# Replacing bf16 idle matmuls at the start of a kernel by about a quarter as many fp32 ones

## The chip, the cores and the metric

The kernel runs on one core of one Trainium2 chip. The metric is device time in microseconds (us) of one execution; the figure quoted is the median of several executions. The span that the profiler shows is about 2 us shorter than that time (403.2 us of 405.02 us in the profiled execution of the kernel before). Ratios and their intervals compare one kernel's fast runs with those of the kernel before in the same rounds, on the same chip, so they are not quite the ratios of the medians.

## The reference

The reference computes Linformer attention (keys and values projected from 1024 rows down to 64) and then a feed-forward layer that takes the maximum of three projections:

```python
def _attn_ref(q, k, v, E, F):            # q, k, v: (8, 8, 1024, 64); E, F: (64, 1024)
    k_proj = np.einsum('ks,bhsd->bhkd', E, k)
    v_proj = np.einsum('ks,bhsd->bhkd', F, v)
    scores = 1.0 / np.sqrt(64) * np.matmul(q, k_proj.transpose(0, 1, 3, 2))
    ...                                  # softmax over the 64 columns
    return np.matmul(attn, v_proj)

def _moe_ref(x, w1, w2, w3, w_out):      # x: (8192, 512); w1..w3: (512, 768); w_out: (768, 512)
    h = np.maximum(np.maximum(x @ w1, x @ w2), x @ w3)
    return (h @ w_out).astype(np.float32)
```

## The kernel before

Apart from `E` and `F`, which come in fp32 by DMAs of SP, everything is loaded in bf16 by DMAs that POOL issues, and PE (TensorE) does nearly all of the work. At the start PE has nothing to compute, as nothing has landed. There the kernel runs matmuls whose result nobody reads, on a zeroed tile `warm`, to keep PE active; the code calls this `idle`. Its purpose is the clock. In this kernel's trace most of the first ten idle matmuls start 0.43 us apart, and those of the second group 0.22 us apart. These two rates are called half and full speed here, and the change from the one to the other the release of the clock.

The parts that matter here, cut:

```python
warm = const.tile([P, 512], BF16, name="warm")
...
nc.vector.memset(warm, 0.0)
make_identity(nc, ident)                     # POOL builds the identity after it has issued six loads
...
def idle(n):
    t, ns = bank()
    for _ in range(n):
        nc.tensor.matmul(out=t, lhsT=warm[:, 0:P], rhs=warm, start=True, stop=True)
    free[ns[0]] = pe(n * MM)                 # the planner's clock only, no instruction
...
idle(10)                                     # the first group
at(6.3)
turn_ef()                                    # casts and transposes E and F: 8 transposes, need ident
q_duo(0)                                     # 16 transposes of q
copy("v", efT[:, :, P:P + KP], efT[:, :, KP:P])
idle(4)                                      # the second group
at(9.0)
k_duo(0)                                     # projection of k_t: 8 matmuls, needs the k_t load
idle(2)
...                                          # scores, softmax sums, further single idle matmuls
up_first(...)                                # the first up-projection, needs the w_sb load
```

The softmax here doesn't subtract the row's maximum and nothing guards it: scores larger than these inputs give would overflow.

Of the kernel before, what the change touches and what calls it, by code (L numbers as in the profile page):

```python
# [8 lines left out]
FP32 = mybir.dt.float32  # L9
# [6 lines left out]
def kernel(  # L16
# [13 lines left out]
    nc = tc.nc  # L30
# [7 lines left out]
    P = 128  # L38
# [11 lines left out]
    const = ctx.enter_context(tc.tile_pool(name="const", bufs=1))  # L50
# [14 lines left out]
    free = [0.0] * 8  # L65
# [13 lines left out]
    def bank():  # L79
        n = min(range(8), key=lambda n: free[n])  # L80
        deal((n,))
        return psum_t[:, n, :], (n,)

    def pe(dt, wait=0.0):
        clock["pe"] = max(clock["pe"], wait) + dt
        return clock["pe"]
# [9 lines left out]
    MM = 0.216  # L96

    def copy(eng, o, i, ns=(), dt=0.65):
        done = {  # L99
            "v": nc.vector.tensor_copy, "s": nc.scalar.copy, "g": nc.gpsimd.tensor_copy  # L100
        }[eng](out=o, in_=i)
        runs(eng, clock["pe"] if ns else 0.0, dt, ns)
        return done
# [14 lines left out]
    ident = const.tile([P, P], BF16, name="ident")  # L118
    ones = const.tile([P, HALF], BF16, name="ones")
    warm = const.tile([P, 512], BF16, name="warm")  # L120
    w_sb = [const.tile([P, NCT, DF], BF16, name=f"w{i}_sb") for i in range(3)]
    wout_sb = const.tile([P, NJT, DO], BF16, name="wout_sb")

# [43 lines left out]
    load_kv(2, slice(2, 4))  # L167

    nc.scalar.preload_act_table_set("natural_log_exp_and_others")
    nc.vector.memset(warm, 0.0)  # L170
    make_identity(nc, ident)
    nc.vector.memset(ones, 1.0)
# [200 lines left out]
        return f  # L373


    def idle(n):

        t, ns = bank()
        for _ in range(n):
            nc.tensor.matmul(out=t, lhsT=warm[:, 0:P], rhs=warm, start=True, stop=True)  # L380
        free[ns[0]] = pe(n * MM)

    def turn_ef():
        for i in range(2):
# [16 lines left out]
    def at(us):  # L401
        clock["pe"] = max(clock["pe"], us)
# [59 lines left out]
    def x(g):  # L462
        scale_x(0, g, *C0, values(0, g, *C0))

    idle(10)
    at(6.3)
    turn_ef()
    q_duo(0)
    copy("v", efT[:, :, P:P + KP], efT[:, :, KP:P])
    idle(4)  # L470
    at(9.0)
    k_duo(0)
    idle(2)
    kt_duo(0)
    idle(1)
# [265 lines left out]
```

## Time and profile before

| | us |
|---|---|
| time, median of 3 (range) | 405.22 (405.04 to 405.93) |
| span of the profiled execution | 403.2 |
| PE busy | 389.6 (97% of the span) |
| first idle group, ten bf16 | 1.20 to 5.38 |
| PE waits for the identity from POOL | 1.21, until 6.58 |
| second idle group, four bf16 | 7.75 to 8.79 |
| PE waits for `k_t` | 1.25, until 10.03 |
| PE waits for `w_sb` | 1.08, until 19.54 |

Two lines of the page of the kernel before: the busy time of each engine, and the chain of work that ended last, by engine.

```profile
PE 389.6 (97%) x2314; PEld 178.0 (44%) x2357; DVE 203.1 (50%) x313; ACT 189.4 (47%) x274; POOL 31.6 (8%) x44
...
PE 82%; DMA 11%; ACT 2%; POOL 1%; DVE 1%; issue 1%; DVEq 0%; ACTq 0%; POOLq 0%
```

Over the whole span PE is the limit. That average does not say what limits the first 20 us, and those are all that the change touches. The same chain in order of time, cut to 0 to 60 us; the columns are start, duration, and what the chain went through:

```profile
1.24 0.88 POOL q_t L152
...
6.48 13.01 DMA w_sb<-in_moe_w_dram
...
25.87 30.10 DMA v_t<-in_v_dram
```

In the front, the chain is POOL issuing loads, then a `w_sb` load on its way until 19.49, and once more a load of the next batch's `v_t`, which lands at 55.97. The front is bound by loads.

The timeline of PE in the front (start, duration of the whole group, engine, line, operation, count, and in brackets the idle time before it and what ended it):

```profile
1.20 4.18 PE L380 MATMUL banks<-warm 128*128 128x512 bf16 x10 [1.20 <-DVE warm L170]
6.58 0.66 PE L391 MATMUL banks<-ident,ef_b 128*128 128x128 bf16 x8 [1.21 <-POOL ident masks.py:199]
...
7.75 1.04 PE L380 MATMUL banks<-warm 128*128 128x512 bf16 x4
10.03 1.03 PE L409 MATMUL banks<-k_t,efT 128*64 128x256 bf16 x8 [1.25 <-DMA k_t<-in_k_dram]
...
19.54 1.47 PE L506 MATMUL banks<-xT,w_sb 128*128 128x512 bf16 x6 [1.08 <-DMA w_sb<-in_moe_w_dram]
```

The three waits in the brackets are gaps that lateness in front of them can use up. The eighth, ninth and tenth idle matmul, one line each:

```profile
4.16 0.63 PE L380 MATMUL banks<-warm 128*128 128x512 bf16 x1
4.58 0.57 PE L380 MATMUL banks<-warm 128*128 128x512 bf16 x1
4.99 0.38 PE L380 MATMUL banks<-warm 128*128 128x512 bf16 x1
```

They start 0.42 to 0.43 us apart until the ninth, which is followed after 0.41 us by a tenth that takes 0.38 us instead of 0.63. In the second group they are 0.22 us apart. So the clock was released to full speed just before 5 us, 3.8 us after PE's first matmul.

What comes before the first idle matmul (timeline of all engines):

```profile
0.86 0.27 DVE L170 MEMSET warm<- 128x256 uint32 x1 [0.86 <-PEq L725]
...
1.24 0.88 POOL L152 DMA_DIRECT2D q_t<-in_q_dram  x1 [0.79 <-POOLq L725]
```

DVE's memset of `warm` lasts from 0.86 to 1.13 us, and POOL issues its first load at 1.24.

### The profile page before, as it was taken

The page shows a single profiled execution, that of the slowest core. Times are in us where ns is not written, and L with a number is a line of the kernel's source. Part 1 is how long each engine was busy: PE and PEld are TensorE (multiplying, and loading weights), DVE is VectorE, ACT ScalarE, POOL GpSimd, SP SyncE. Part 2 cuts the span into 40 slices and gives each one's busy share as a digit, 9 for nine tenths or more (in the row PEclk, how much of TensorE's full clock was granted, in tenths as well). Part 3 has the DMA queues.
Part 4 walks back from the last instruction along what each step waited for, and adds up shares of the span by engine and source line. Part 5 has one row for each costly group of instructions (what it writes and reads, how often), then busy time and mean ns, then how long its engine had stood idle before and what let it go on. Part 6 is the DMA issues. An engine that isn't in the chain of part 4 may idle for free.

```text
span 403.2 us, 5841 instructions
## 1 busy us (share of the span) xinstructions
PE 389.6 (97%) x2314; PEld 178.0 (44%) x2357; DVE 203.1 (50%) x313; ACT 189.4 (47%) x274; POOL 31.6 (8%) x44
## 2 busy tenths in 40 slices
PE   6799999999999999999999999999999999999996
PEld 2444444344444435444544445444544444444443
DVE  2338755761764527537353655626364363525251
ACT  2622537525672376555643555437535555432322
POOL 7340001001000100100100002000000000000000
PEclk9999999999999999999999999999999999999999
DMA  9999999959907994991799029950510202020202
GB/s 150 206 205 207 232 201 165 235 128 187 227 0 216 191 220 106 155 243 20 211 178 216 24 40 236 204 148 0 147 63 2 104 2 104 2 104 0 106 0 105
DMA packets 62667, 53.33 MB, mean 132 GB/s; under 512 B 30128, under 2 KB 58288, under 8 KB 62640
## 3 DMA queue, kind: packets, MB, share of 16 engines
q0 software_dynamic: 28512, 28.31, 44.3%
q1 hardware_dynamic: 33984, 24.51, 19.7%
q8 instruction: 18, 0.29, 0.3%
q10 hardware_dynamic: 144, 0.13, 0.1%
q14 instruction: 9, 0.07, 0.1%
HBM read 57.15 MB, written 16.78 MB: 183 GB/s over the span
## 4 chain that ended last, share of the span: by engine, by line
PE 82%; DMA 11%; ACT 2%; POOL 1%; DVE 1%; issue 1%; DVEq 0%; ACTq 0%; POOLq 0%
PE banks L506 56%; PE banks L603 18%; DMA v_t<-in_v_dram 7%; PE banks L220 4%; DMA w_sb<-in_moe_w_dram 3%; PE banks L284 3%; PE banks L200 2%; DVE xT L250 1%; ACT zi L239 1%; ACT zl L233 1%; DMA out_dram<-o_sb 0%; POOL k_t L147 0%; POOL q_t L152 0%; POOL v_t L147 0%; PE banks L435 0%
## 5 line engine op out<-in xcount | busy, mean ns | idle before, releaser
L506 PE MATMUL banks<-xT,w_sb 128*128 128x512 bf16 x1119 | 254.9, 379 | 3.7 <-DMA w_sb<-in_moe_w_dram 1.1
L506 PEld LDWEIGHTS <-w_sb 128*128 128x128 bf16 x1152 | 109.4, 98 | 138.1 <-issue 10.7
L568 DVE TENSOR_TENSOR m<-banks,h1s 128x512 f32<-128x512 f32 x90 | 62.1, 690 | 84.4 <-ACT h1s L564 52.2
L564 ACT COPY h1s<-banks 128x512 f32<-128x512 f32 x90 | 52.5, 583 | 90.3 <-PE banks L506 88.2
L603 PE MATMUL banks<-wout_sb,hT 128*128 128x512 bf16 x370 | 84.6, 379 | 0.8 <-issue 0.5
L250 DVE TENSOR_TENSOR xT<-banks,zi 128x1024 bf16<-128x1024 f32 (+1 forms) x36 | 39.8, 1106 | 73.6 <-ACT zi L239 54.2
L516 DVE TENSOR_TENSOR hT<-banks,m 128x512 bf16<-128x512 f32 x90 | 62.3, 692 | 10.4 <-PE banks L506 1.2
L99 ACT COPY o_sb<-banks 128x512 f32<-128x512 f32 (+1 forms) x56 | 32.6, 581 | 52.2 <-PE banks L603 52.1
L603 PEld LDWEIGHTS <-hT 128*128 128x128 bf16 x378 | 36.0, 98 | 45.2 <-issue 3.1
L233 ACT ACTIVATE zl<-banks 128x1024 f32<-128x1024 f32 (+1 forms) x36 | 33.5, 930 | 31.4 <-PE banks L220 30.5
L211 ACT ACTIVATE pT<-banks 128x1024 bf16<-128x1024 f32 (+1 forms) x36 | 33.2, 930 | 15.6 <-PE banks L200 15.6
L239 ACT ACTIVATE zi<-zl 128x1024 f32<-128x1024 f32 (+1 forms) x36 | 34.6, 962 | 1.1
L189 POOL DMA_DIRECT2D q_t<-in_q_dram x7 | 6.2, 880 | 201.0 <-DMA qT<-q_p 70.6
L220 PE MATMUL banks<-pT,ones 64*64 64x512 bf16 (+1 forms) x144 | 13.7, 374 | 0.7 <-DVE xT L250 0.3
L220 PE MATMUL banks<-pT,vp 64*64 64x512 bf16 (+1 forms) x144 | 13.3, 355 | 0.7 <-DVE vp L99 0.6
L200 PE MATMUL banks<-qT,kpT 64*64 64x512 bf16 (+1 forms) x144 | 13.3, 358 | 0.6 <-DVE m L568 0.3
L284 PEld LDWEIGHTS <-efT 128*64 128x64 bf16 x224 | 11.6, 110 | 3.3 <-issue 2.7
L99 DVE CAST vp<-banks 64x256 bf16<-64x256 f32 (+1 forms) x18 | 7.1, 397 | 7.4 <-ACT vp L99 3.7
L220 PEld LDWEIGHTS <-ones 64*64 64x64 bf16 x144 | 4.4, 103 | 14.3 <-issue 14.2
L99 DVE COPY q_p<-q_t 128x1024 bf16<-128x1024 bf16 x28 | 10.0, 419 | 0.0
L99 ACT CAST vp<-banks 64x256 bf16<-64x256 f32 x14 | 5.1, 365 | 8.8 <-PE banks L284 8.6
L380 PE MATMUL banks<-warm 128*128 128x512 bf16 x19 | 7.0, 498 | 1.2 <-DVE warm L170 1.2
(48 smaller groups left out, 102.5 us busy)
## 6 DMA issues: line engine op xcount, KB each, us to landing
out_dram<-o_sb SPq DMA_DIRECT2D x30, 512.0 KB, 3.4
q_t<-in_q_dram POOLq DMA_DIRECT2D x7, 1024.0 KB, 9.6
k_t<-in_k_dram POOLq DMA_DIRECT2D x7, 1024.0 KB, 14.0
v_t<-in_v_dram POOLq DMA_DIRECT2D x7, 1024.0 KB, 18.8
w_sb<-in_moe_w_dram POOLq DMA_DIRECT2D x5, 384.0 KB, 12.4
k_t<-in_k_dram POOLq DMA_DIRECT2D x2, 512.0 KB, 9.1
v_t<-in_v_dram POOLq DMA_DIRECT2D x4, 256.0 KB, 12.2
wout_sb<-in_moe_w_out_dram POOLq DMA_DIRECT2D x1, 768.0 KB, 15.7
```

What stands on the lines that cost most here:

```text
L99: done = {"v": nc.vector.tensor_copy, "s": nc.scalar.copy, "g": nc.gpsimd.tensor_copy}[eng](out=o, in_=i)
L211: nc.scalar.activation(out=pTs[b, g, lo], in_=t, func=AF.Exp, scale=scale)
L220: nc.tensor.matmul(out=t[hp * HALF:(hp + 1) * HALF, c, 0:nsi * HALF], lhsT=w(rows, hp), rhs=p[rows, hp, :], start=True, stop=True,)
L233: nc.scalar.activation(out=zl, in_=t, func=AF.Ln)
L239: nc.scalar.activation(out=zi, in_=zl, func=AF.Exp, scale=-1.0)
L250: nc.vector.tensor_tensor(out=xTs[b][:, g, lo:lo + nsi, :].rearrange("a (c s) p -> a c (s p)", c=2), in0=t, in1=zi, op=ALU.mult,)
L284: nc.tensor.matmul(out=t[hh * HALF:(hh + 1) * HALF, 0:width], lhsT=efT[:, si, (kv - 1) * KP:kv * KP], rhs=qkv[b][kv][:, heads[hh], si, :], ...
L506: nc.tensor.matmul(out=h, lhsT=w_sb[i][:, ct, jt * P:(jt + 1) * P], rhs=xTs[b][:, ct, ch * SPC:(ch + 1) * SPC, :], start=(ct == first), st ...
L516: nc.vector.tensor_tensor(out=o, in0=h, in1=other, op=ALU.max)
L564: nc.scalar.copy(out=h1s, in_=h[0][0])
L568: nc.vector.tensor_tensor(out=m12, in0=h[1][0], in1=h1s, op=ALU.max)
L603: nc.tensor.matmul(out=o_ps, lhsT=hTs[b, ch][:, jt, tt * P:(tt + 1) * P], rhs=wout_sb[:, jt, :], start=(jt == 0), stop=(jt == NJT - 1),)
```

## The change

The idle matmuls at the front become fp32 ones, about a quarter as many. The intent is to keep PE as active with fewer instructions. The changed planner counts an fp32 one as four bf16 ones. No trace of the kernel before has an fp32 matmul; the profile after shows one at half speed as two instructions 0.85 us apart, so about 1.7 us, four times the 0.43 us of a bf16 one. Ten become three (as long as 12 bf16 ones) and four become one (as long as 4). The later idle matmuls stay bf16, so both tiles are needed, and the new memset stands first.

```diff
+    warm_f = const.tile([P, 512], FP32, name="warm_f")
 ...
+    nc.vector.memset(warm_f, 0.0)
     nc.vector.memset(warm, 0.0)
 ...
-    def idle(n):
+    def idle(n, w=warm):
 ...
-            nc.tensor.matmul(out=t, lhsT=warm[:, 0:P], rhs=warm, start=True, stop=True)
-        free[ns[0]] = pe(n * MM)
+            nc.tensor.matmul(out=t, lhsT=w[:, 0:P], rhs=w, start=True, stop=True)
+        free[ns[0]] = pe(n * MM * (4 if w is warm_f else 1))
 ...
-    idle(10)
+    idle(3, warm_f)
 ...
-    idle(4)
+    idle(1, warm_f)
```

## The prediction

> **What bounds the kernel now.** The median is 405.22 us (405.04 to 405.93), the span 403.2 us. The page has PE busy 389.6 us (97%), and the chain that ended last is 82% PE. But the edit touches only the first 9 us, and there the chain is not PE: it runs through POOL issuing loads (1.24 to 6.24 us, with the identity build at its end), then the DMA of a `w_sb` piece (6.48 to 19.49). Then the first up-projection matmul starts (19.54, after PE idled 1.08 us). So the front is bound by loads.
>
> **What the idle matmuls do now (timeline).** Ten bf16 128x512 from `warm` run from 1.20 to 5.38. They start 0.43 us apart (weight loads at 1.60, 2.03 ... 4.59), nine of about 0.61 us; the last must be about 0.38 us, as the mean is 600 ns. So the array reached full speed near 5.0 us. The PEclk row (1.00 throughout) doesn't show this. PE then waits 1.21 us for the identity from POOL and starts the transposes at 6.58. Four more idle matmuls run 7.75 to 8.79, about 0.22 us apart. PE then waits 1.25 us for `k_t` (10.03).
>
> **What the change does.**
> - DVE gets one more memset, 128x512 fp32, in front. The 128x256 one took 0.272 us and 128x64 took 0.112: about 0.83 ns an element, so 0.49 us by estimate. The first idle matmul starts at 1.41 to 1.5 instead of 1.20. POOL's first load issue (1.24) should not move.
> - 3 fp32 matmuls replace 10, 1 replaces 4. [...]
> - With the release after as much activity as now (3.8 us, near 5.2 us), three finish near 6.1, range 5.7 to 6.6[...].
> - Nothing else moves; the bank order is unchanged.
>
> **Critical path.** Ending by 6.58 costs nothing. Ending at 7.9 delays transposes and `efT` copies by 1.3 us, about all of the 1.24 us wait for `k_t`. Anything left meets the 1.08 us wait before 19.54. Filling the gap from 5.4 to 6.6 buys nothing: the clock is already full by 5.0. I expect 0.0 us of effect on the path, give or take 0.5 us of DMA timing.
>
> **Prediction: 405.3 us, 80% range 404.5 to 406.2.** Faster by over 2%: 0.01; within 2%: 0.98; slower by over 2%: 0.01.
>
> **What would show it.** Right: the first fp32 matmul at 1.4 to 1.5, spans of about 1.7 us then shorter, transposes at 6.6 to 7.0 with full-speed durations (eight in about 0.66 us), the first `k_t` matmul at 10.0, the first up-projection matmul at 19.5, and the stretch from 20 us on unchanged. Wrong: transposes or `k_t` projection at twice their duration (fp32 passes don't release the clock), POOL's first issue later than 1.24 (the memset holds it up, which shifts the loads).
>
> **What would make it wrong.** If the clock isn't released by fp32 activity, everything up to some 10 us runs slower, up to 2 us by estimate, about half hidden behind the `w_sb` wait: 406 to 407 us.

Three fp32 matmuls of about 1.7 us at half speed, begun at 1.41 to 1.5 us and sped up by a release near 5.2, finish near 6.1 us. The upper case is the end at 7.9 us under "Critical path".

## The result and the profile after

The changed kernel took 405.28 us (median of 5, 405.19 to 405.52), and the kernel before took 405.29 us (median of 5, 405.04 to 405.93). The ratio is 0.9998 with a 95% interval from 0.9984 to 1.0013: the same.

The page of the changed kernel, same lines as before:

```profile
PE 394.5 (98%) x2351; PEld 178.5 (44%) x2351; DVE 203.5 (50%) x314; ACT 189.4 (47%) x274; POOL 31.6 (8%) x44
...
PE 82%; DMA 11%; ACT 2%; DVE 1%; POOL 1%; issue 1%; DVEq 0%; ACTq 0%; POOLq 0%
```

PE's busy sum is 4.9 us higher at the same time, and this must not be read as more work. The page before counts 1119 up-projection matmuls and 1152 weight loads for them, so some matmul records are missing there.

The memset and POOL's first issue (timeline of all engines):

```profile
0.92 0.48 DVE L171 MEMSET warm_f<- 128x512 f32 x1 [0.92 <-PEq L727]
...
1.25 0.88 POOL L153 DMA_DIRECT2D q_t<-in_q_dram  x1 [0.80 <-POOLq L727]
```

The new memset takes 0.48 us and ends at 1.40. POOL's first issue stays at 1.25: the memset holds up nothing but the idle matmuls.

PE in the front, with the lines that answer to those before:

```profile
1.46 5.28 PE L382 MATMUL banks<-warm_f 128*128 128x512 f32 x6 [1.46 <-DVE warm_f L171]
6.58 0.66 PE L393 MATMUL banks<-ident,ef_b 128*128 128x128 bf16 x8
...
7.74 1.12 PE L382 MATMUL banks<-warm_f 128*128 128x512 f32 x2
9.90 1.03 PE L411 MATMUL banks<-k_t,efT 128*64 128x256 bf16 x8 [1.04 <-DMA k_t<-in_k_dram]
...
19.50 1.47 PE L508 MATMUL banks<-xT,w_sb 128*128 128x512 bf16 x6 [1.18 <-DMA w_sb<-in_moe_w_dram]
```

There are two lessons in the first line. Three fp32 matmuls are six records: each fp32 matmul runs as two instructions. And the group ends at 6.74, after the first transpose has begun, so it fills the 1.21 us wait for the identity to its end. From the transposes on, all is as it was: 6.58, 7.74, then `k_t` at 9.90, and the first up-projection matmul at 19.50 (19.54 before). Single records of the first group:

```profile
4.18 1.06 PE L382 MATMUL banks<-warm_f 128*128 128x512 f32 x1
5.03 1.06 PE L382 MATMUL banks<-warm_f 128*128 128x512 f32 x1
5.89 0.85 PE L382 MATMUL banks<-warm_f 128*128 128x512 f32 x1
```

Instructions of the group start 0.85 us apart, twice the 0.43 us of a bf16 one, up to the last; that one begins at 5.89, and the first transpose follows 0.69 us later. The clock was therefore released in the sixth instruction, near 6.4 us, not near 5. The chain, in order of time, is the one from before:

```profile
6.48 12.97 DMA w_sb<-in_moe_w_dram
...
25.95 30.06 DMA v_t<-in_v_dram
```

### The profile page after: what moved, and what is told of

Read it like the earlier page. It is cut to its first block, busy times and chain, and to the rows that moved or that the text cites. A ratio compares the mean times of both kernels' runs of the same rounds, so it can differ in the third digit from the quotient of the medians.

```text
span 403.5 us, 5873 instructions
## 1 busy us (share of the span) xinstructions
PE 394.5 (98%) x2351; PEld 178.5 (44%) x2351; DVE 203.5 (50%) x314; ACT 189.4 (47%) x274; POOL 31.6 (8%) x44
## 4 chain that ended last, share of the span: by engine, by line
PE 82%; DMA 11%; ACT 2%; DVE 1%; POOL 1%; issue 1%; DVEq 0%; ACTq 0%; POOLq 0%
PE banks L508 56%; PE banks L605 18%; DMA v_t<-in_v_dram 7%; PE banks L222 4%; DMA w_sb<-in_moe_w_dram 3%; PE banks L286 3%; PE banks L202 2%; ACT zi L241 1%; DVE xT L252 1%; ACT zl L235 1%; DMA out_dram<-o_sb 0%; POOL k_t L148 0%; POOL q_t L153 0%; POOL v_t L148 0%; DVE m L570 0%
## 5 line engine op out<-in xcount | busy, mean ns | idle before, releaser
L508 PE MATMUL banks<-xT,w_sb 128*128 128x512 bf16 x1152 | 257.9, 379 | 1.5 <-DMA w_sb<-in_moe_w_dram 1.2
L605 PE MATMUL banks<-wout_sb,hT 128*128 128x512 bf16 x378 | 85.7, 379 | 0.1
L99 DVE COPY o_sb<-banks 128x512 f32<-128x512 f32 (+1 forms) x9 | 5.8, 654 | 4.5 <-DMA out_dram<-o_sb 4.5
```

What stands on the lines that cost most here:

```text
L99: done = {"v": nc.vector.tensor_copy, "s": nc.scalar.copy, "g": nc.gpsimd.tensor_copy}[eng](out=o, in_=i)
L508: nc.tensor.matmul(out=h, lhsT=w_sb[i][:, ct, jt * P:(jt + 1) * P], rhs=xTs[b][:, ct, ch * SPC:(ch + 1) * SPC, :], start=(ct == first), st ...
L605: nc.tensor.matmul(out=o_ps, lhsT=hTs[b, ch][:, jt, tt * P:(tt + 1) * P], rhs=wout_sb[:, jt, :], start=(jt == 0), stop=(jt == NJT - 1),)
```

## The experiments

Theory A, the prediction's: both kernels release the clock in time, and the front has slack because it waits for loads, so nothing of the change is on the path. Its rivals:

- B: there is no slack, every microsecond of idle matmul counts, and the tie is two effects that cancel.
- C (named in the expectation of fp32_x8): the front does not matter at all, as later load waits absorb whatever happens there.
- E: these idle matmuls are worth nothing, whatever their type.
- D: fp32 matmuls count for less as activity, so fp32 releases the clock later (6.4 against 5.0 us above).
- F: the release point differs from execution to execution, and the two points above are chance.

In every experiment the planner's clock values were kept, so that the order of all other work and its PSUM banks stay those of the changed kernel (before_again is the kernel before itself). Each kernel gave correct results. "Before" was timed on the same chip: its medians were 405.54 us (11 runs), 404.97 (9) and 405.07 (11). Kernels are compared only within the same rounds.

| run | first, second group | median us (range) | ratio to before, 95% interval |
|---|---|---|---|
| fp32_x8 | 8 fp32, 1 fp32 | 407.27 (406.94 to 408.49) | 1.0046 (1.0028 to 1.0064) |
| bf16_x32 | 32 bf16, 1 fp32 | 407.97 (406.87 to 408.40) | 1.0053 (1.0035 to 1.0071) |
| no_front | none, none | 407.00 (406.13 to 408.85) | 1.0038 (1.0016 to 1.0060) |
| fp32_x2 | 2 fp32, 1 fp32 | 406.03 (405.50 to 406.39) | 1.0008 (0.9991 to 1.0025) |
| before_again | 10 bf16, 4 bf16 | 405.12 (404.99 to 405.31) | 1.0000 (0.9986 to 1.0013) |
| after_again | 3 fp32, 1 fp32 | 405.35 (405.22 to 406.56) | 1.0010 (0.9996 to 1.0023) |
| bf16_x12 | 12 bf16, 4 bf16 | 405.48 (405.17 to 405.68) | 1.0007 (0.9995 to 1.0020) |
| fp32_x4 | 4 fp32, 1 fp32 | 405.50 (405.39 to 406.61) | 1.0014 (1.0001 to 1.0026) |
| no_front_again | none, none | 406.73 (406.04 to 407.21) | 1.0032 (1.0016 to 1.0047) |
| no_first | none, 1 fp32 | 405.77 (405.32 to 406.50) | 1.0011 (0.9995 to 1.0028) |
| no_second | 3 fp32, none | 406.19 (405.22 to 409.01) | 1.0032 (1.0004 to 1.0060) |
| bf16_x12_again | 12 bf16, 4 bf16 | 405.72 (405.18 to 406.19) | 1.0003 (0.9987 to 1.0020) |

### Is there slack? Eight fp32 ones, and the same work as bf16

```diff
-    idle(3, warm_f)
+    idle(8, warm_f, plan=12)        # run fp32_x8; plan: what the planner is told
```

> Eight fp32 idle matmuls in front instead of three (16 half-instructions from 1.46 us). Theory A (the front is hidden behind loads, with a slack of 1.04 us before the k_t projection plus 1.18 us before the first up-projection matmul): about 5.8 halves at 0.853 us until the clock is full near 6.4, the rest at 0.43, so the group ends near 10.8 and the transposes start near 10.6, 4.0 us late; 4.0 minus 2.2 leaves +1.8 us (407.1). Rival B (no slack, each microsecond of idle matmul counts): +4.0 us (409.3). Rival C (the front doesn't matter at all before 19.5 us of loads and also later waits absorb it): within 0.4 us of before.

```diff
-    idle(3, warm_f)
+    idle(32, warm_b, plan=12)       # run bf16_x32; warm_b is warm_f read as bf16
```

> The same array work as the run with eight fp32 ones, 32 bf16 matmuls with the same start (they read the zeroed fp32 tile as bf16). If fp32 and bf16 release the clock alike (the later release in the changed kernel was chance or phase), release near 5.0 to 6.4 us in both and the same time within 0.5 us. If fp32 activity counts for less (theory D), the release is near 5.2 us here against 6.4 with fp32, and this run is about 0.6 us faster. Total by theory A: +1.2 to +1.8 us on before.

PE in the front of fp32_x8:

```profile
1.46 10.09 PE L382 MATMUL banks<-warm_f 128*128 128x512 f32 x16 [1.46 <-DVE warm_f L171]
11.38 0.65 PE L395 MATMUL banks<-ident,ef_b 128*128 128x128 bf16 x8
...
13.59 1.06 PE L413 MATMUL banks<-k_t,efT 128*64 128x256 bf16 x8
...
21.97 1.74 PE L510 MATMUL banks<-xT,w_sb 128*128 128x512 bf16 x6
```

Read each line against the changed kernel's. The transposes are late by 4.80 us (11.38 against 6.58), the `k_t` projection by 3.69 (13.59 against 9.90), the first up-projection matmul by 2.47 (21.97 against 19.50). At each of the two load waits about 1.1 to 1.2 us of lateness vanishes, and the brackets that named these waits are gone: PE no longer arrives before the loads.

But the start of the first up-projection does not show the whole lateness. Its six matmuls take 1.74 us here and 1.47 in the changed kernel, and the `v_t` projection behind them waits for `zl`, which ACT (ScalarE) computes. First the changed kernel, then fp32_x8:

```profile
20.80 0.61 PE L437 MATMUL banks<-v_t,efT 128*128 128x128 bf16 x8
...
23.97 0.61 PE L439 MATMUL banks<-v_t,efT 128*128 128x128 bf16 x8 [0.26 <-ACT zl L235]
```

That is 3.17 us late, close to the 2.97 us by which this execution was longer than the profiled one of the changed kernel (408.49 and 405.52 us). So from the `k_t` projection on only about 0.5 us of lateness was absorbed (3.69 to 3.17), though the wait for `w_sb` was 1.18: once PE comes later than the load, the chain through `zl` is what it waits for next. The slack of the front is about 1.6 us (4.80 less 3.17), not the sum of the two load waits, 2.2.

The median time rose by 1.73 us over that of before, and the ratio comes to 1.9 us. Theory A had said +1.8, B +4.0, and C within 0.4, so B and C fall. That the median is so near to +1.8 is in part luck, as A's sum took 2.2 us of slack. The profiled execution was the slowest of the six. Here the front is on the path.

The bf16 run gave the same within the error (ratios 1.0046 and 1.0053, with intervals that overlap). It also gave the first sign against D. The two records in which its matmuls go from half to full speed:

```profile
6.56 0.63 PE L382 MATMUL banks<-warm_f 128*128 128x512 bf16 x1
6.98 0.42 PE L382 MATMUL banks<-warm_f 128*128 128x512 bf16 x1
```

The matmul of 0.63 us is the last at half speed; the one at 6.98 takes 0.42 and is the first that is faster (the next starts at 7.24, 0.26 us later instead of 0.43). So this bf16 group was released near 7.1 us, later than the three fp32 ones were. In fp32_x8 the release was near 7.45.

### Are the idle matmuls worth anything? Leave them out

```diff
-    idle(3, warm_f)
+    idle(0, warm_f, plan=12)
 ...
-    idle(1, warm_f)
+    idle(0, warm_f, plan=4)         # runs no_front and no_front_again
```

> Both front groups of idle matmuls emit nothing (planner unchanged). Theory A says that the two kernels tie because both release the clock before 6.58 us; without any, the transposes at 6.58 and the k_t projection at 9.9 run at half speed (1.7 us instead of 0.85 for the eight of k_t), the clock is released only some 4 us into the work after 9.9, and the first up-projection matmul moves from 19.5 to about 20.5 to 21.5: +1 to +2 us (406.3 to 407.3). Rival E (these idle matmuls are worth nothing, whatever their type, as loads bound the front): within 0.4 us of before.

> Both front groups emit nothing, once more: in its first profile k_t landed 1.1 us later (11.06 us) than in the profiles of the two kernels, so its +1.5 us was not the clock's alone. Theory A (missing clock release): k_t projection at half speed (eight in 1.86 us) again wherever k_t lands, full speed only near 15 us, time +1 to +2 us on before. If the first result was only a late k_t: within 0.5 us of before when k_t lands near 10.

The median rose by 1.5 us (ratio 1.0038) and in the repeat by 1.7 us (1.0032); both intervals exclude 1, so E falls. The first profile was no clean proof, as `k_t` landed only at 11.06 in it. In the second it landed at 9.66, earlier than in the changed kernel, so a late load is not the cause there:

```profile
6.47 1.01 PE L395 MATMUL banks<-ident,ef_b 128*128 128x128 bf16 x8 [6.47 <-POOL ident masks.py:199]
...
9.66 1.87 PE L413 MATMUL banks<-k_t,efT 128*64 128x256 bf16 x8 [1.19 <-DMA k_t<-in_k_dram]
...
16.21 1.06 PE L413 MATMUL banks<-k_t,efT 128*64 128x256 bf16 x8
...
20.35 1.74 PE L510 MATMUL banks<-xT,w_sb 128*128 128x512 bf16 x6
```

The first `k_t` projection takes 1.87 us, and the identical second one, when the clock has been released, 1.06. The first up-projection matmul follows at 20.35 instead of 19.50, and waits for no load. The `v_t` projection behind it waits for `zl`, as in fp32_x8, and starts at 22.35 instead of 20.80. These 1.55 us are close to the 1.32 us by which this execution was longer than the profiled one of the changed kernel (406.84 and 405.52 us).

### How few are enough?

```diff
-    idle(3, warm_f)
+    idle(2, warm_f, plan=12)        # run fp32_x2
```

> Two fp32 idle matmuls in front instead of three: they end near 5.0 us, 1.4 us before the clock was seen to be released with three. If release needs about 4.9 us of fp32 activity, the transposes at 6.58 run at half speed (eight in about 1.1 us instead of 0.66), the later single fp32 one runs cold or finishes the release near 8 to 9 us; the k_t wait of 1.04 us hides that: total within 0.5 us of before. If release comes after 3.8 us of activity or by phase, the transposes run at full speed. Rival B (no slack): +1 us.

```profile
7.47 0.71 PE L395 MATMUL banks<-ident,ef_b 128*128 128x128 bf16 x8 [2.23 <-ACT ef_b L99]
...
10.58 1.86 PE L413 MATMUL banks<-k_t,efT 128*64 128x256 bf16 x8 [0.28 <-DMA k_t<-in_k_dram]
```

In this execution, `E` and `F` landed late (the transposes waited for the cast until 7.47, so PE stood idle for 2.2 us). The eight transposes took 0.71 us, near full speed, but the `k_t` projection then took 1.86 us: the clock was full for a while and half again (by the clock records of the trace, which are explained below, it was full from 5.75 to 9.16 us and half until 12.58). The time is not clearly different (1.0008, interval from 0.9991 to 1.0025). What the two fp32 ones do in an execution with early loads is left open.

### Type against chance: both kernels again, and type alone undone

```diff
-    idle(3, warm_f)
+    idle(12, warm_b, plan=12)
 ...
-    idle(1, warm_f)
+    idle(4, warm_b, plan=4)         # runs bf16_x12 and bf16_x12_again: same start, four bf16 for each fp32
```

> The kernel before once more, for a second look at where the clock is released. So far, release was at 4.97 us with ten bf16 (PE active since 1.20), at about 6.4 with three fp32, at 7.07 with 32 bf16 and at 7.45 with eight fp32 (all three active since 1.46). Theory F: the release point varies from execution to execution by some 2.5 us, whatever the type. Then this profile may show another release point than 4.97, and in executions where it would fall after 5.4 us, where the ten matmuls end, the projections of the front run at half speed. Theory D (fp32 releases later, bf16 at a fixed 3.8 us): release again near 5.0. Time: ratio to before within 0.15% of 1.

> The changed kernel once more. Theory F: a release point other than 6.4 us is likely; its fp32 matmuls keep PE active to 6.58, where the transposes begin, so fewer executions miss the release than before, and the spread of its times should be no wider than that of before (404.74 to 406.75 in the last call). Theory D: release again within 0.2 us of 6.4. Time: within 0.3% of before.

> The changed kernel's array work and start (1.46 us) with bf16 matmuls in place of fp32 ones: 12 and 4. Type alone is undone. Theory A and F (type is of no account): within 0.3% of before, transposes at 6.6 to 6.8. If fp32 has a cost of its own (exposed weight loads, later release) this is up to 0.3 us faster than the changed kernel in the same call, which is about what five rounds can see.

> Type alone undone, once more, for another release point with bf16 (so far 4.97, between 5.4 and 6.5, about 6.6, 7.07; with fp32 6.2, about 6.4, about 7.4, 7.45) and another comparison of times. Theory F: anywhere from 5.0 to 7.5 us. Time within 0.3% of before; 1.0007 last time.

The kernel before, profiled a second time, first the timeline of PE and then the tenth idle matmul alone:

```profile
1.19 4.45 PE L380 MATMUL banks<-warm 128*128 128x512 bf16 x10 [1.19 <-DVE warm L170]
6.47 0.66 PE L391 MATMUL banks<-ident,ef_b 128*128 128x128 bf16 x8 [0.83 <-POOL ident masks.py:199]
...
9.91 1.03 PE L409 MATMUL banks<-k_t,efT 128*64 128x256 bf16 x8 [1.24 <-DMA k_t<-in_k_dram]
```

```profile
5.01 0.63 PE L380 MATMUL banks<-warm 128*128 128x512 bf16 x1
```

This is the same kernel as at the top of this document, and the tenth matmul now takes 0.63 us where it took 0.38. All ten ran at half speed, and the clock was released only in the gap between 5.64 and 6.47, for the eight transposes then take 0.66 us. The changed kernel, profiled a second time:

```profile
1.46 5.49 PE L382 MATMUL banks<-warm_f 128*128 128x512 f32 x6 [1.46 <-DVE warm_f L171]
6.74 0.98 PE L393 MATMUL banks<-ident,ef_b 128*128 128x128 bf16 x8
...
9.80 1.03 PE L411 MATMUL banks<-k_t,efT 128*64 128x256 bf16 x8 [0.46 <-DMA k_t<-in_k_dram]
```

Here the release came later still. The transposes take 0.98 us instead of 0.66 and end near 7.7; the second group pays for that with the wait before `k_t`, 0.46 us instead of 1.04, and `k_t` starts at 9.80. This is the slack of theory A at work inside the changed kernel itself.

All release points, read from the spacing of matmuls (where the release falls inside an instruction, it is placed by splitting the spacing between half and full speed):

| type | release, us from the span's start | us after PE's first matmul |
|---|---|---|
| bf16 | 4.97; 5.6 to 6.5; 6.07; about 6.6; 7.1 | 3.8; 4.5 to 5.3; 4.6; 5.1; 5.6 |
| fp32 | 5.1; 6.2; about 6.4; about 7.4; 7.45 | 3.6; 4.7; 4.9; 5.9; 6.0 |

fp32_x2 is left out, as PE stood idle from 5.24 to 7.47 us there. The points of the two types overlap over nearly the whole range (3.8 to 5.6 us and 3.6 to 6.0 us). D's fixed points (5.0 for bf16, 6.4 for fp32) are refuted by the repeats, and F holds: the release point moves by 2.1 us between executions with bf16 and by 2.4 us with fp32. Whether fp32 is later on average by some tenths of a microsecond, ten points cannot say. The times agree: with bf16 at the same start and four bf16 matmuls for each fp32 one the ratios to before are 1.0007 and 1.0003, with fp32 0.9998 and 1.0010. Type makes no difference that these runs can see.

What F calls chance can be read from the packed traces. They keep the records of the granted clock one by one, where `prof` shows only a mean over a stretch. These records confirm the table: the clock becomes full at 4.97, 5.80, 6.06, 6.55 and 7.05 us with bf16, and at 5.07, 6.17, 6.40, 7.43 and 7.51 us with fp32. So the release differs between executions in the clock's own records as well, by 2.1 us with bf16 and by 2.4 us with fp32. What sets the instant was not shown.

F's further guess, that the changed kernel has fewer slow executions than before because its group lasts to the transposes, was not borne out: after_again had one execution above 406 us in five (406.56), the changed kernel's first five had none, and before had five in 31 (406.27 to 406.75). What made these slow ones was not profiled.

### A longer group as insurance

```diff
-    idle(3, warm_f)
+    idle(4, warm_f, plan=12)        # run fp32_x4
```

> Four fp32 matmuls in front instead of three: PE is active without a break from 1.46 until the transposes, which start at 7.3 to 8.3 us according to the release point. Theory A: k_t lands at 9.9 to 11.1 us in the five profiles so far and the work between takes 2.3 us, so 7.6 to 8.8 would still be early enough: within 0.3% of before. If theory F holds and before misses the release in some executions, this has no slow tail: median 0.1 to 0.5 us below before. Rival B (no slack): +0.7 to +1.7 us.

It is 0.6 us slower (1.0014, interval from 1.0001 to 1.0026), a small loss in place of the small gain that F would have allowed. Its profile still shows a wait of 0.85 us before `k_t`, so the loss was not traced to one wait and stays open. The changed kernel was at 1.0010 in the same call, so the fourth matmul itself is not shown to cost anything. No version beat the kernel before.

### Which of the two groups does the work?

```diff
-    idle(3, warm_f)
+    idle(0, warm_f, plan=12)        # run no_first
```

> Only the first group (three fp32) is left out; the single fp32 one after the q transposes stays. Theory A: PE has too little activity before k_t lands for the release, so about as slow as without both: +1 to +2 us. If one group is enough: within 0.5 us of before.

```profile
6.58 1.01 PE L395 MATMUL banks<-ident,ef_b 128*128 128x128 bf16 x8 [6.58 <-POOL ident masks.py:199]
...
8.52 2.01 PE L382 MATMUL banks<-warm_f 128*128 128x512 f32 x2
10.46 1.06 PE L413 MATMUL banks<-k_t,efT 128*64 128x256 bf16 x8
...
18.84 1.74 PE L510 MATMUL banks<-xT,w_sb 128*128 128x512 bf16 x6
```

The expectation failed: 1.0011 (0.9995 to 1.0028), not +1 to +2 us. The transposes ran at half speed (1.01 us), and the single fp32 matmul too (2.01 us); but that slow matmul filled the wait for `k_t`, and the clock had been released by the time it ended (by its record at 10.33 us). The `k_t` projection took 1.06 us. The slow fp32 matmul kept PE busy for 2.01 us, where the same one took 1.12 us in the changed kernel. This, too, is one profile.

```diff
-    idle(1, warm_f)
+    idle(0, warm_f, plan=4)         # run no_second
```

> Only the second group (one fp32) is left out: PE then stands idle from about 7.8 us to the landing of k_t at 9.8 to 11. If the clock survives 2 us or more without work: k_t projection at full speed (1.03 us), within 0.3% of before. If it drops, the projection takes 1.86 us and the time is +0.5 to +1.5 us. It also gives another release point for three fp32 ones (6.4 and about 7.4 so far).

```profile
10.45 1.03 PE L413 MATMUL banks<-k_t,efT 128*64 128x256 bf16 x8 [2.65 <-DMA k_t<-in_k_dram]
...
12.21 0.61 PE L382 MATMUL banks<-warm 128*128 128x512 bf16 x1
...
16.12 1.92 PE L413 MATMUL banks<-k_t,efT 128*64 128x256 bf16 x8
...
21.47 1.74 PE L510 MATMUL banks<-xT,w_sb 128*128 128x512 bf16 x6
```

Without the second group PE stood idle for 2.65 us before `k_t`, which landed at 10.45 in this execution. The projection still ran at full speed, but soon afterwards the clock fell: the idle bf16 matmul at 12.21 takes 0.61 us, and the second `k_t` projection 1.92 us. The first up-projection matmul starts at 21.47, 1.97 us late, and the `v_t` projection behind it at 23.47, 2.67 us late. Two stretches of the same run in the view of busy time by windows (the last three figures of a line are the granted clock, the DMA share and GB/s):

```profile
2.00:5.00 3.00, 3.00 (x4) 1.01 (x3) 0.00 (x0) 0.02 (x1) 3.00 (x5) 1.00 1.06 216
...
12.00:16.00 4.00, 4.00 (x38) 1.72 (x37) 0.92 (x2) 2.25 (x4) 1.38 (x3) 0.50 1.24 206
```

The record gives the clock as 0.50 from 12 to 16 us, but as 1.00 from 2 to 5 us, where fp32 instructions 0.85 us apart show half speed as well. The fall of the clock is recorded, the slow start is not: the trace's first clock record starts with the release, at 5.07, and the view counts the time before it as full speed. By the records the clock fell at 11.90, 1.45 us after work had resumed, and came back only at 18.72, although PE's timeline shows no wait between 10.45 and 19.3 us. Why it did not come back sooner is open. In fp32_x2 a gap of 2.23 us was followed by a fall at 9.16, 1.69 us after work had resumed; after the gaps of 1.24 us in before_again and 1.43 us in bf16_x12_again the `k_t` projection took 1.03 us, and the mean granted clock of both executions is 1.000. These are single profiles. The median is +1.1 us and the mean +1.3 us (1.0032). This execution, 407.95 us, was one of the slow ones of a wide spread (405.22 to 409.01). Of the two groups, only leaving out the second gave a loss clear of noise; the two intervals overlap, so which of them is worth more is not settled.

## Why the prediction was right

- **The time.** Predicted 405.3 us (404.5 to 406.2), measured 405.28. The effect on the path was predicted as zero, and the ratio is 0.9998.
- **What bounds the front.** Loads, as predicted. The run fp32_x8 shows it by using up the slack: 4.80 us of lateness became 3.17 at the `v_t` projection behind the first up-projection. The wait for `k_t` absorbed about 1.1 us (it was 1.04). The wait before 19.54, 1.08 us, which the prediction counted as slack as well, was worth only about 0.5, because PE then waits for `zl`. The change used none of this second slack, so the error did not show.
- **The length of an fp32 matmul.** Predicted 1.7 us for each at half speed; measured 2 x 0.85 us. Not foreseen: they are two instructions, each with its own weight load, of 0.33 us at half speed against 0.15 us for a bf16 one.
- **The memset.** Predicted 0.49 us and a start of 1.41 to 1.5; measured 0.48 us and 1.46. POOL's first issue stayed at 1.25.
- **The release of the clock** is the term that was mis-sized. The prediction took 3.8 us of activity from one trace and put the release near 5.2 us and the end of the group near 6.1, within 5.7 to 6.6. It ended at 6.74, with the release near 6.4; in the repeat, the release came near 7.4, and the transposes ran slow for a while, which the prediction listed as a sign that fp32 does not release the clock. It was not: the release varies by 2.1 us with bf16 and by 2.4 us with fp32. One profile gave a number that is no constant. The error cost nothing, since the predicted slack of 1.24 us before `k_t` covered it.
- **What a missing release would cost.** Predicted 406 to 407 us; with no idle matmuls at the front, no_front and no_front_again took 407.00 and 406.73. That is not quite the predicted case, as nothing keeps PE active there, but the clock is missing in the same place.

## What to carry to other kernels

Before you tune filler work at the start, read which load the first real matmul waits for, and measure the slack by making the filler longer until the time moves. Do not add up the waits instead: when one is used up, the next work can be held by something else, as in fp32_x8, where the two load waits added up to 2.2 us and the slack was about 1.6. Try a short group that bridges a later load wait as well as a long one at the start: here the ratio was 1.0032 (from 1.0004) without the second group and 1.0011 (from 0.9995) without the first, with intervals that overlap. Their type made no difference that these runs can see (bf16 1.0007 and 1.0003, fp32 0.9998 and 1.0010, with four bf16 matmuls for each fp32 one). Never take the release point of one profile as a constant: in ten it lay 3.6 to 6.0 us after PE's first matmul.
